# Starting a hand-written engine order three units earlier, and a vote in two steps

## The chip, the cores and the metric

One core of a Trainium2 chip. The metric is the device time of one execution in microseconds, the median of several runs.

## What is computed

```python
state = np.zeros((B, H, D, D))                      # (4, 8, 48, 48)
for t in range(S):                                  # 768
    kt, vt, rt, wt = (k[:, :, t], v[:, :, t], r[:, :, t], w[:, :, t])
    cur = np.einsum('bhd,bhe->bhde', u[None] * kt, vt)
    y[:, :, t] = np.einsum('bhd,bhde->bhe', rt, state + cur)
    state = wt[:, :, :, None] * state + np.einsum('bhd,bhe->bhde', kt, vt)
x = y.transpose(0, 2, 1, 3).reshape(B * S, H * D)   # (3072, 384)
h = x @ w_in                                        # w_in (384, 2048)
out = (h * np.cos(h)) @ w_out                       # w_out (2048, 384)
```

A linear attention with a decaying state, and behind it a two-layer network whose gate is h cos h. All of it is in float32.

## The kernel before

**Chunks.** The sequence is cut into 24 chunks of 128 steps (4 batches of 6). For each chunk the tile tt holds r, k and w; v and rk (r and k once more, with time on the partitions) are loaded apart. `att_decay` turns the decays into products: e, a backward scan on VectorE (L225); f, a reciprocal and a forward scan (L230, L232); then r and k are multiplied by the scans' results (steps r, L237, and k, L238). `att_diag` makes the diagonal of the scores: m and u multiply rk by k and by u (L250, L251), c sums over each head (L255), and GpSimd spreads the sums out (L265). TensorE computes scores (pa, L288), transposes of k (pt, L301; step K copies them to kn), the new state (pst, L323; step n adds the old one) and the outputs (py, L355 to L374); P puts the scores into their triangle (L292), X splits the outputs in a high and a low part, xT (L148). The step d multiplies the state of the chunk before (L278), and four small copies on ScalarE place it in past.

**Units.** Two chunks make a block of 256 columns of the network, and a block has 8 units of 256 columns of w_in. For a unit t, mm1 makes ph with 18 matmuls in three passes of split precision (L443); the gate follows: I rounds (ScalarE, L405), S reduces (VectorE, L408), N is the sine (ScalarE, L421), M multiplies with ph (VectorE, L422), H takes the high part (ScalarE, L145) and L the low part (GpSimd, L148, two instructions). mm2 then adds 12 matmuls to acc (L462), two units later (`LAG`). Only two PSUM banks hold ph in this part, so mm1 of unit t waits for M of unit t-2.

**Weights.** Each pair of weight blocks is loaded raw and split by ScalarE and VectorE (lines 155 to 176) once, in the first 106 us, between units 0 and 15, which belong to blocks 0 and 1 in the order `PAIR`.

**Order.** In the rows `START` the events of the first units are written out, by hand for TensorE alone; the other engines' order there comes from the scheduler, by priorities. After `START` the order of TensorE, VectorE, ScalarE and GpSimd is the order of the code, and SyncE's is the scheduler's. There `events` reads one row of `PLAN` for each unit t; "k+5" is step k of chunk 2i + 5, where i is t // 8; e, m and the like put a part of a step at that place, and t+2 has TensorE transpose a chunk. Before, `START` has five rows that end with unit 15, and the rows by hand begin with unit 16; only its third (n = 2) differs from `PLAN`. The dictionaries `EARLY` and `LATER` say which engine does what in the two phases: in `EARLY` rk is multiplied on GpSimd and kn copied on ScalarE, in `LATER` both on VectorE.

**Vote.** At the end the largest |w| and the smallest product of decays decide whether the result stands or a slow loop runs. `take_vote` is called behind unit slots-4: VectorE makes vote, least and low (L568 to L572), TensorE sums them over the partitions (L574, L575), VectorE makes a number of it.

Of the kernel before, what the change touches and what calls it, by code (L numbers as in the profile page):

```python
# [9 lines left out]
F32 = mybir.dt.float32  # L10
# [7 lines left out]
ALU = mybir.AluOpType  # L18
ET = mybir.EngineType

C = 128
# [4 lines left out]
R = ROW + HD  # L26
# [26 lines left out]
PLAN = ["t+2 t+3 load+6 mm1 K+2 K+3 e+4 I S k+4 N M mm2 H L f+4",  # L53
# [7 lines left out]
START = ["load0 load1 f lv0 decay0 f diag0 a0 lv1 decay1 diag1 a1 w load2 f w o0 x0 decay2 diag2 m0 m1",  # L61
# [4 lines left out]
FIRST = {2: "mm1 a+2 a+3 I S m+4 N M P+2 P+3 mm2 H L"}  # L66
LAST = "mm1 I S N M", "mm1 I S N M mm2 h l", "mm2 h l"
CHECK = 14
PAIR = "0001110101010101"
# [1 line left out]
             o="a lv", s="t d lv", p="o d")  # L71
# [3 lines left out]
def rwkv_cos_ffn(ctx: ExitStack, tc: tile.TileContext, tr, tn, tv, u, ut, wts, w, rkw, vst, us, xs, out):  # L75
    nc = tc.nc
# [8 lines left out]
    cst = ctx.enter_context(tc.tile_pool(name="cst", bufs=1))  # L85
# [6 lines left out]
    def bank(kind, shape, name):  # L92

        tags = BANKS[stage[0]]
        turn[kind] += 1
        return ps.tile(shape, F32, tag=tags[kind][turn[kind] % len(tags[kind])], name=name)
# [3 lines left out]
    def buf(tag, shape, dtype, name=None, pool=sb):  # L100
# [16 lines left out]
                            axis=mybir.AxisListType.X, op=ALU.add)  # L117
# [5 lines left out]
    ones = cst.tile([128, 1], F32, name="ones")  # L123
# [7 lines left out]
    raw, wgt, last = {}, {}, {}  # L131

    E = {}
# [256 lines left out]
    def check_decays(n):  # L390

        ww = buf("tt", [128, w.shape[1] // WCH], F32, "ww")
        nc.sync.dma_start(out=ww, in_=w[:, n * w.shape[1] // WCH:(n + 1) * w.shape[1] // WCH])
        top = buf("top", [128, 1], F32)
        nc.vector.tensor_reduce(out=top, in_=ww, axis=mybir.AxisListType.X, op=ALU.max, apply_absolute_value=True)
        nc.vector.tensor_tensor(out=wmax, in0=wmax, in1=top, op=ALU.max)
# [86 lines left out]
    NU = NF // FU  # L483
# [3 lines left out]
    for i in PAIR:  # L487
# [3 lines left out]
    slots = len(seq)  # L491
# [4 lines left out]
                 a=att_scores, t=att_transpose, s=att_state, o=att_own, p=att_past, x=att_x)  # L496
# [37 lines left out]
    def up(n):  # L534

        if n == 0 and up1[0] < slots:
            if up1[0] - up1[1] > LAG + 1:
                up(1)
            mm1(up1[0])
            up1[0] += 1  # L540
        elif n == 1 and up1[1] < up1[0]:
            mm2(up1[1])
            up1[1] += 1

    def events(i, row, t):
        for e in row.split():
            n, _, d = e.partition("+")
            if e == "mm1":
                up(0)
            elif e == "mm2":  # L550
                if up1[1] <= t - LAG:
                    up(1)
            elif e in "ISNMHLhl":
                at = (e.upper(), t - e.islower())
                if at in parts:
                    parts.pop(at)()
            elif n in "efrkmucPKXn":
                at = i * (1 if n in "Xn" else BLK) + int(d)
                for m in dict(e=("decay",), m=("diag",)).get(n, ()):
                    att(at, m)  # L560
                if (n, at) in parts:
                    parts.pop((n, at))()
            else:
                att(i * (1 if n in "osp" else BLK) + int(d), n)

    def take_vote():
        vote = cst.tile([128, 1], F32, name="vote")
        nc.vector.tensor_single_scalar(out=vote, in_=wmax, scalar=1.0, op=ALU.is_gt)  # L568
        least = cst.tile([R, 1], F32, name="least")
        nc.vector.tensor_reduce(out=least, in_=wholes.rearrange("p g a -> p (g a)"), axis=mybir.AxisListType.X, op=ALU.min)  # L570
        low = cst.tile([R, 1], F32, name="low")
        nc.vector.tensor_single_scalar(out=low, in_=least, scalar=LEAST, op=ALU.is_le)  # L572
        pv = bank("a", [C, 512], "pv")
        nc.tensor.matmul(out=pv[:1, 0:1], lhsT=vote, rhs=ones[:, 0:1], start=True, stop=True)  # L574
        nc.tensor.matmul(out=pv[:1, 1:2], lhsT=ones[:R, 0:1], rhs=low, start=True, stop=True)  # L575
        votes = cst.tile([1, 1], F32, name="votes")
        nc.vector.tensor_reduce(out=votes, in_=pv[:1, 0:2], axis=mybir.AxisListType.X, op=ALU.add)
        nc.vector.tensor_copy(out=bad, in_=votes)

    bad = cst.tile([1, 1], I32, name="bad")  # L580

    up1 = [0, 0]
# [15 lines left out]
    with tc.manual_schedule(engines={ET.PE, ET.DVE, ET.Activation, ET.Pool}):  # L598
        up2 = up1[0]
        for t in range(up2, slots + LAG):  # L600
            n = t % NU
            if t == slots - 2:
                E["g0"] = nc.vector
            row = FIRST[n] if t < up2 + NU and n in FIRST else PLAN[n]
            events(t // NU, row if t < slots - 2 else LAST[t - slots + 2] if t <= slots else "mm2", t)
            if t >= slots - CHECK and n_checked[0] < WCH:
                check_decays(n_checked[0])
                n_checked[0] += 1
            if t == slots - 4:
                take_vote()  # L610
        while up1[1] < slots:
            up(1)
    assert not parts, list(parts)
# [159 lines left out]
```

## Time and profile before

| what | value |
|---|---|
| median of 3 runs | 538.82 us (538.73 to 540.53) |
| the profiled execution, its own time | 538.93 us |
| its span in the profile | 537.2 us |
| TensorE busy | 503.7 us, 94% |
| VectorE busy | 378.9 us, 71% |
| ScalarE busy | 274.2 us, 51% |
| GpSimd busy | 212.9 us, 40% |

The span reaches from the first to the last instruction; the 1.7 us between it and the execution's own time lie around it. Busy is the time in which the engine executes something, as a share of the span. An engine that is not busy may wait for another one, and a busy engine may be busy with nothing that the end waits for, so the shares alone don't say which engine sets the time.

### The profile page before, as it was taken

The page shows a single profiled execution, that of the slowest core. Times are in us where ns is not written, and L with a number is a line of the kernel's source. Part 1 is how long each engine was busy: PE and PEld are TensorE (multiplying, and loading weights), DVE is VectorE, ACT ScalarE, POOL GpSimd, SP SyncE. Part 2 cuts the span into 40 slices and gives each one's busy share as a digit, 9 for nine tenths or more (in the row PEclk, how much of TensorE's full clock was granted, in tenths as well). Part 3 has the DMA queues.
Part 4 walks back from the last instruction along what each step waited for, and adds up shares of the span by engine and source line. Part 5 has one row for each costly group of instructions (what it writes and reads, how often), then busy time and mean ns, then how long its engine had stood idle before and what let it go on. Part 6 is the DMA issues. An engine that isn't in the chain of part 4 may idle for free.

```text
span 537.2 us, 11909 instructions
## 1 busy us (share of the span) xinstructions
PE 503.7 (94%) x4964; PEld 485.7 (90%) x4964; DVE 378.9 (71%) x570; ACT 274.2 (51%) x454; POOL 212.9 (40%) x274
## 2 busy tenths in 40 slices
PE   3657999969999999999999999999999999999997
PEld 3656898958999999999999999999999999999987
DVE  7998999864746946946946946946946946678433
ACT  1788999635535435444434435435434444444543
POOL 4161346744323524524524524524524524423320
PEclk9878999999999999999999999999999999999999
DMA  8994851214142132133132123123123120050000
GB/s 272 315 322 133 270 188 57 63 60 136 64 116 54 60 109 59 60 96 74 60 95 74 60 79 91 60 70 100 59 63 115 60 97 23 31 177 1 31 2 32
DMA packets 16728, 52.17 MB, mean 97 GB/s; under 512 B 2016, under 2 KB 8416, under 8 KB 16672
## 3 DMA queue, kind: packets, MB, share of 16 engines
q1 hardware_dynamic: 16528, 51.28, 31.1%
q8 instruction: 40, 0.66, 0.5%
q14 instruction: 16, 0.13, 0.1%
q10 hardware_dynamic: 144, 0.10, 0.1%
HBM read 46.65 MB, written 4.72 MB: 96 GB/s over the span
## 4 chain that ended last, share of the span: by engine, by line
PE 77%; DVE 13%; ACT 4%; issue 2%; POOL 2%; DMA 1%; DVEq 0%; ACTq 0%; POOLq 0%
PE ph L443 33%; PE acc L462 32%; PE pa L288 4%; DVE h L173 2%; PE py L355 2%; DVE w L148 2%; PE py L360 2%; PE pst L323 2%; DVE rr L422 1%; DVE ee L225 1%; DVE tt L232 1%; PE py L374 1%; DVE rr L408 1%; PE pt L301 1%; DVE tt L237 1%
## 5 line engine op out<-in xcount | busy, mean ns | idle before, releaser
L148 POOL TENSOR_TENSOR gs<-rr,gs 128x256 fp32r<-128x256 f32 x188 | 155.1, 846 | 245.4 <-ACT gs L145 245.4
L443 PE MATMUL ph<-xT,w 128*128 128x256 f32 x1728 | 224.4, 284 | 11.5 <-ACT w L145 5.2
L443 PEld LDWEIGHTS ph<-xT,w 128*128 128x128 f32 x1728 | 215.2, 190 | 15.6 <-ACT w L145 5.6
L462 PE MATMUL acc<-w,gs 128*128 128x384 f32 x1152 | 217.3, 338 | 1.1 <-DVE rr L422 1.0
L462 PEld LDWEIGHTS acc<-w,gs 128*128 128x128 f32 x1152 | 195.9, 188 | 2.5 <-issue 1.2
L408 DVE SCALAR_TENSOR_TENSOR rr<-rr,ph 128x512 f32<-128x512 int32 x96 | 65.6, 683 | 85.3 <-ACT rr L405 84.8
L421 ACT ACTIVATE rr<-rr,quarter 128x512 f32<-128x512 f32 x96 | 69.4, 723 | 89.8 <-DVE rr L408 89.6
L145 ACT CAST gs<-rr 128x512 fp32r<-128x512 f32 x96 | 59.6, 621 | 66.3 <-DVE rr L422 39.1
L422 DVE TENSOR_TENSOR rr<-rr,ph 128x512 f32<-128x512 f32 x96 | 65.7, 684 | 29.1 <-ACT rr L421 29.0
L405 ACT ACTIVATE rr<-ph 128x512 int32<-128x512 f32 x96 | 57.3, 597 | 54.3 <-PE ph L443 53.7
L265 POOL TENSOR_SCALAR_AFFINE_SELECT asb<-cd 128x512 f32<-128x512 f32 x48 | 42.8, 915 | 60.4 <-DVE cd L255 40.9
L225 DVE TENSOR_TENSOR_SCAN ee<-tt,one_e 112x516 f32<-112x516 f32 x24 | 33.1, 1381 | 1.6 <-DMA tt<-tr 1.6
L292 DVE COPY_PREDICATED asb<-mask,pa 128x512 f32<-128x512 uint8 x48 | 31.7, 727 | 1.3 <-PE pa L288 1.3
L148 DVE TENSOR_TENSOR xT<-py,xT 128x384 fp32r<-128x384 f32 x24 | 12.2, 551 | 26.1 <-ACT xT L145 26.1
L232 DVE TENSOR_TENSOR_SCAN tt<-tt,inj 112x516 f32<-112x516 f32 x24 | 30.1, 1254 | 0.6
L288 PE MATMUL pa<-tt 48*128 48x128 f32 x384 | 28.2, 299 | 0.0
L288 PEld LDWEIGHTS pa<-tt 48*128 48x128 f32 x384 | 25.0, 205 | 2.8 <-issue 2.2
L244 PEld LDWEIGHTS pc<-u_by_head,rkt 112*128 112x128 f32 x48 | 8.3, 262 | 14.7 <-DVE rkt L219 8.4
L244 PE MATMUL pc<-u_by_head,rkt 112*128 112x2 f32 x48 | 8.7, 303 | 13.5 <-DVE rkt L219 12.9
L237 DVE TENSOR_TENSOR tt<-tt 112x512 f32<-112x512 f32 x24 | 21.0, 875 | 0.1
L145 ACT COPY past<-dd 48x192 f32<-48x192 f32 x40 | 14.0, 350 | 13.7 <-DVE dd L278 11.3
L238 DVE TENSOR_TENSOR tt<-tt,ee 112x512 f32<-112x512 f32 x24 | 20.0, 835 | 0.0
(68 smaller groups left out, 345.6 us busy)
## 6 DMA issues: line engine op xcount, KB each, us to landing
tt<-tr SPq DMA_DIRECT2D x22, 674.2 KB, 7.0
raw<-wts SPq DMA_DIRECT2D x16, 768.0 KB, 6.0
rk<-tn SPq DMA_DIRECT2D x18, 384.0 KB, 3.3
v<-tv SPq DMA_DIRECT2D x24, 224.0 KB, 5.9
ww<-w SPq DMA_DIRECT2D x6, 768.0 KB, 5.1
out<-ob SPq DMA_DIRECT2D x23, 192.0 KB, 2.0
tt<-tr SPq DMA_DIRECT2D x4, 224.0 KB, 4.7
tt<-tr SPq DMA_DIRECT2D x2, 226.2 KB, 3.8
```

The costliest lines, as they stand in the source:

```text
L145: (nc.scalar.copy if E[name] is nc.scalar else E[name].tensor_copy)(out=out, in_=in_)
L148: E[name].tensor_tensor(out=out, in0=full, in1=high.bitcast(F32), op=ALU.subtract)
L225: nc.vector.tensor_tensor_scan(out=ee.rearrange("p a t -> p (a t)")[:, ::-1], data0=wp[:, 1:W129 + 1][:, ::-1], data1=one_e.rearrange("p a ...
L232: nc.vector.tensor_tensor_scan(out=wp[:, 0:W129], data0=wp[:, 0:W129], data1=inj.rearrange("p a t -> p (a t)"), initial=0.0, op0=ALU.mult, ...
L265: nc.gpsimd.affine_select(out=asb, in_=col.unsqueeze(2).to_broadcast([C, NP, C]), pattern=[[0, 4], [1, C]], compare_op=ALU.is_equal, fill= ...
L288: nc.tensor.matmul(out=pa[h][:, p], lhsT=a["k3"][rows(h), p], rhs=a["r3"][rows(h), p], start=True, stop=True)
L405: nc.scalar.activation(made["rr"].bitcast(I32), ph, AF.Copy, scale=INV2PI / W_SCALE, bias=0.25)
L408: nc.vector.scalar_tensor_tensor(out=made["rr"], in0=made["rr"].bitcast(I32), scalar=-2.0 * math.pi * W_SCALE, in1=ph, op0=ALU.mult, op1=A ...
L421: N=lambda: nc.scalar.activation(made["rr"], made["rr"], AF.Sin, scale=1.0 / W_SCALE, bias=quarter),
L422: M=lambda: nc.vector.tensor_tensor(out=made["rr"], in0=made["rr"], in1=ph, op=ALU.mult), H=high, L=low)
L443: nc.tensor.matmul(out=ph[:, fi], lhsT=wgt[u * FU + fi][:, 0, a, kt * 128:(kt + 1) * 128], rhs=xT[:, b, kt], start=n == 0, stop=n == 3 * K ...
L462: nc.tensor.matmul(out=accs[i][j][:, :DM], lhsT=gs[:, a, fi, j * C:(j + 1) * C], rhs=wgt[u * FU + fi][:, 1, b], start=u == 0 and fi == 0 a ...
```

## The change

The fifth row of `START` is taken away, so that the order by hand begins with unit 13. `FIRST` becomes a list of seven rows for units 13 to 19, and from unit 20 on `PLAN` is used. The copies kn are made on ScalarE in units 13 to 15. `take_vote` is split: the operations of VectorE come behind unit slots-5, the matmuls and what follows behind unit slots-4, as before.

```diff
-         "mm2 m0 m1 lr6 lr7 diag6 decay6 mm2 t4 t5 m0 m1 lv6 lv7 diag7 decay7 s2 mm2 o2 p2 load8 lr8 lr9 m0 m1 x4 mm2 load9 d6 d7 lv8 lv9"]
-FIRST = {2: "mm1 a+2 a+3 I S m+4 N M P+2 P+3 mm2 H L"}
+FIRST = ["mm2 lr+4 lr+5 mm1 load+6 I S e+4 N M mm2 H L k+4",
+         "t+2 t+3 mm1 K+2 K+3 f+4 I S s+1 n+1 N M mm2 H L r+4 m+4 u+4",
+         "o+1 p+1 mm1 load+7 c+4 lr+6 X+1 I S e+5 N M mm2 H L k+5 f+5 m+5 lv+6 lv+7 d+4 d+5",
+         "t+2 t+3 mm1 K+2 K+3 r+3 I S u+3 N M mm2 H L c+3 lr+5 load+6 e+4",
...
-    def take_vote():
+    def take_vote(last):
+        if last:
+            pv = bank("a", [C, 512], "pv")
+            nc.tensor.matmul(out=pv[:1, 0:1], lhsT=told["vote"], rhs=ones[:, 0:1], start=True, stop=True)
+            nc.tensor.matmul(out=pv[:1, 1:2], lhsT=ones[:R, 0:1], rhs=told["low"], start=True, stop=True)
...
+            return
...
-            n = t % NU
+            n = t - up2
+            E["kn"] = nc.scalar if n < 3 else nc.vector
...
-            row = FIRST[n] if t < up2 + NU and n in FIRST else PLAN[n]
+            row = FIRST[n] if n < len(FIRST) else PLAN[t % NU]
...
-            if t == slots - 4:
-                take_vote()
+            if t in (slots - 5, slots - 4):
+                take_vote(t == slots - 4)
```

TensorE's order is the same instruction for instruction. In the changed kernel all lines behind the table stand 5 lines lower (L408 is L413, L422 is L427, L225 is L230, L238 is L243), those behind `take_vote` 9.

First place: VectorE between the gates of units 11 and 13, before. rr_1068 is unit 11, rr_1133 unit 12 and rr_1195 unit 13; tt_1162 is chunk 7, rk_1206 its rk.

```order
L422 TENSOR_TENSOR rr_1068<-rr_1068,ph_1049 128x512
L225 SCALAR_TENSOR_TENSOR ee_1289<-tt_1162,one_e_77 112x516
L255 TENSOR_REDUCE cd_1283<-rk_1206 128x8
L230 RECIPROCAL inj_80<-ee_1289 112x4
L238 TENSOR_TENSOR tt_1162<-tt_1162,ee_1289 112x512
L232 SCALAR_TENSOR_TENSOR tt_1162<-tt_1162,inj_80 112x516
L237 TENSOR_TENSOR tt_1162<-tt_1162 112x512
L408 SCALAR_TENSOR_TENSOR rr_1133<-rr_1133,ph_1114 128x512
L422 TENSOR_TENSOR rr_1133<-rr_1133,ph_1114 128x512
L408 SCALAR_TENSOR_TENSOR rr_1195<-rr_1195,ph_1176 128x512
```

The same place in the changed kernel (rr_1204 is unit 13, tt_1099 chunk 6):

```order
L427 TENSOR_TENSOR rr_1068<-rr_1068,ph_1049 128x512
L297 COPY_PREDICATED asb_1035<-mask_75,pa_1088 128x512
L413 SCALAR_TENSOR_TENSOR rr_1133<-rr_1133,ph_1114 128x512
L427 TENSOR_TENSOR rr_1133<-rr_1133,ph_1114 128x512
L413 SCALAR_TENSOR_TENSOR rr_1204<-rr_1204,ph_1183 128x512
L230 SCALAR_TENSOR_TENSOR ee_1207<-tt_1099,one_e_77 112x516
L427 TENSOR_TENSOR rr_1204<-rr_1204,ph_1183 128x512
```

Six instructions of chunk 7 between M of unit 11 and S of unit 12 are gone, the sum over rk among them, whose products GpSimd made; chunk 6's backward scan, which stood ahead of unit 8's M, comes in unit 13.

Second place: VectorE from the gate of unit 15 on, before (rr_1419 is unit 15, kn_1486 and kn_1488 the transposed k of chunks 6 and 7) and then in the changed kernel (rr_1401 is unit 15).

```order
L408 SCALAR_TENSOR_TENSOR rr_1419<-rr_1419,ph_1400 128x512
L422 TENSOR_TENSOR rr_1419<-rr_1419,ph_1400 128x512
L145 COPY kn_1486<-pt_1455 128x384
L145 COPY kn_1488<-pt_1460 128x384
L225 SCALAR_TENSOR_TENSOR ee_1490<-tt_1392,one_e_77 112x516
```

```order
L413 SCALAR_TENSOR_TENSOR rr_1401<-rr_1401,ph_1367 128x512
L230 SCALAR_TENSOR_TENSOR ee_1404<-tt_1162,one_e_77 112x516
L427 TENSOR_TENSOR rr_1401<-rr_1401,ph_1367 128x512
L243 TENSOR_TENSOR tt_1162<-tt_1162,ee_1404 112x512
L235 RECIPROCAL inj_80<-ee_1404 112x4
L237 SCALAR_TENSOR_TENSOR tt_1162<-tt_1162,inj_80 112x516
L255 TENSOR_TENSOR rk_1181<-rk_1181 128x384
L283 TENSOR_TENSOR dd_1433<-sn_773,ee_1207 112x192
L283 TENSOR_TENSOR dd_1437<-sn_775,ee_1404 112x192
L150 COPY kn_1470<-pt_1441 128x384
L150 COPY kn_1472<-pt_1446 128x384
```

Chunk 7's scan, its multiplication of k, which TensorE transposes at the start of unit 16, and seven more instructions now stand around M of unit 15.

Third place: VectorE around the vote, before (rr_6046 is unit slots-4) and in the changed kernel (rr_6052).

```order
L422 TENSOR_TENSOR rr_6006<-rr_6006,ph_5987 128x512
L408 SCALAR_TENSOR_TENSOR rr_6046<-rr_6046,ph_6027 128x512
L422 TENSOR_TENSOR rr_6046<-rr_6046,ph_6027 128x512
L568 TENSOR_SCALAR vote_6067<-wmax_87 128x1
L570 TENSOR_REDUCE least_6069<-wholes_86 112x1
L572 TENSOR_SCALAR low_6071<-least_6069 112x1
L577 TENSOR_REDUCE votes_6076<-pv_6073 1x1
```

```order
L427 TENSOR_TENSOR rr_6006<-rr_6006,ph_5987 128x512
L581 TENSOR_SCALAR vote_6027<-wmax_87 128x1
L583 TENSOR_REDUCE least_6029<-wholes_86 112x1
L585 TENSOR_SCALAR low_6031<-least_6029 112x1
L413 SCALAR_TENSOR_TENSOR rr_6052<-rr_6052,ph_6033 128x512
L427 TENSOR_TENSOR rr_6052<-rr_6052,ph_6033 128x512
L577 TENSOR_REDUCE votes_6076<-pv_6073 1x1
```

Three operations moved from behind unit slots-4's gate to ahead of it.

## Rows read from the trace of the kernel before

**Rows 1.** Windows: busy us and instructions per engine, TensorE's clock, DMA share, GB/s.

```profile
88.00:124.00 36.00, 29.32 (x238) 26.90 (x237) 27.55 (x40) 19.90 (x34) 22.50 (x22) 1.00 0.22 67
151.00:172.00 21.00, 21.00 (x267) 20.30 (x266) 12.37 (x21) 9.04 (x17) 7.40 (x10) 1.00 0.40 108
```

**Rows 2.** TensorE's timeline, 88 to 122 us: start, duration, instruction, [idle before, releaser].

```profile
88.83 2.35 PE L462 MATMUL acc<-w,gs 128*128 128x384 f32 x12
91.36 2.37 PE L443 MATMUL ph<-xT,w 128*128 128x256 f32 x18 [0.18 <-DVE rr L422]
94.34 1.05 PE L244 MATMUL pc<-u_by_head,rkt 112*128 112x2 f32 x8 [0.62 <-DVE asb L292]
...
105.00 2.25 PE L462 MATMUL acc<-w,gs 128*128 128x384 f32 x12
108.42 2.34 PE L443 MATMUL ph<-xT,w 128*128 128x256 f32 x18 [1.17 <-DVE rr L422]
110.59 2.92 PE L462 MATMUL acc<-w,gs 128*128 128x384 f32 x12
113.36 0.93 PE L301 MATMUL pt<-ident,tt 112*128 112x112 f32 x8
117.48 2.36 PE L443 MATMUL ph<-xT,w 128*128 128x256 f32 x18 [3.19 <-DVE rr L422]
120.46 0.67 PE L323 MATMUL pst<-v,kn 128*64 128x48 f32 x16 [0.62 <-ACT kn L145]
121.90 0.67 PE L323 MATMUL pst<-v,kn 128*64 128x48 f32 x16 [0.78 <-ACT kn L145]
```

**Rows 3.** TensorE's timeline in an undisturbed stretch, 170 to 174 us.

```profile
170.56 2.25 PE L462 MATMUL acc<-w,gs 128*128 128x384 f32 x12
172.65 0.93 PE L301 MATMUL pt<-ident,tt 112*128 112x112 f32 x8
173.35 2.35 PE L443 MATMUL ph<-xT,w 128*128 128x256 f32 x18
```

**Rows 4.** VectorE's timeline, four rows between 96 and 117 us.

```profile
96.89 1.78 DVE L232 TENSOR_TENSOR_SCAN tt<-tt,inj 112x516 f32<-112x516 f32 x1
...
108.20 1.22 DVE L225 TENSOR_TENSOR_SCAN ee<-tt,one_e 112x516 f32<-112x516 f32 x1
111.35 0.55 DVE L255 TENSOR_REDUCE cd<-rk 128x8 f32<-128x384 f32 x1 [1.93 <-POOL rk L251]
...
116.65 0.69 DVE L422 TENSOR_TENSOR rr<-rr,ph 128x512 f32<-128x512 f32 x1 [0.79 <-ACT rr L421]
```

**Rows 5.** GpSimd's timeline at 96.8 us, the two subtractions of a gate.

```profile
96.76 2.45 POOL L148 TENSOR_TENSOR gs<-rr,gs 128x256 fp32r<-128x256 f32 x2 [2.42 <-ACT gs L145]
```

**Rows 6.** The timeline of all engines near the end, around the vote.

```profile
510.95 2.26 PE L443 MATMUL ph<-xT,w 128*128 128x256 f32 x18
...
512.74 1.43 POOL L148 TENSOR_TENSOR gs<-rr,gs 128x256 fp32r<-128x256 f32 x2 [2.76 <-ACT gs L145]
...
513.05 2.25 PE L462 MATMUL acc<-w,gs 128*128 128x384 f32 x12
...
513.95 0.69 DVE L408 SCALAR_TENSOR_TENSOR rr<-rr,ph 128x512 f32<-128x512 int32 x1 [2.02 <-ACT rr L405]
...
516.24 0.19 PE L574 MATMUL pv<-ones,vote 128*1 128x1 f32 x2 [0.94 <-DVE vote L568]
...
516.59 0.19 PE L575 MATMUL pv<-low,ones 112*1 112x1 f32 x2 [0.16 <-DVE low L572]
...
516.70 2.37 PE L443 MATMUL ph<-xT,w 128*128 128x256 f32 x18
```

**Rows 7.** VectorE's groups by line and shape, 125 to 500 us: busy, mean ns | idle before.

```profile
L225 DVE TENSOR_TENSOR_SCAN ee<-tt,one_e 112x516 f32<-112x516 f32 x16 | 21.9, 1367 | 0.0
...
L238 DVE TENSOR_TENSOR tt<-tt,ee 112x512 f32<-112x512 f32 x16 | 13.2, 825 | 0.0
```

**Rows 8.** DMA issues of the page: KB each, median us to landing.

```profile
tt<-tr SPq DMA_DIRECT2D x22, 674.2 KB, 7.0
```

More of the change, by code (lines that the diff above doesn't have):

```diff
@@ L564, in events @@
                 att(i * (1 if n in "osp" else BLK) + int(d), n)
-    def take_vote():
-        vote = cst.tile([128, 1], F32, name="vote")
+    def take_vote(last):
[3 more added lines that the diff above has]
+            nc.tensor.matmul(out=pv[:1, 1:2], lhsT=ones[:R, 0:1], rhs=told["low"], start=True, stop=True)
+            votes = cst.tile([1, 1], F32, name="votes")
+            nc.vector.tensor_reduce(out=votes, in_=pv[:1, 0:2], axis=mybir.AxisListType.X, op=ALU.add)
+            nc.vector.tensor_copy(out=bad, in_=votes)
+            return
+        told["vote"] = vote = cst.tile([128, 1], F32, name="vote")
         nc.vector.tensor_single_scalar(out=vote, in_=wmax, scalar=1.0, op=ALU.is_gt)
@@ L570, in take_vote @@
         nc.vector.tensor_reduce(out=least, in_=wholes.rearrange("p g a -> p (g a)"), axis=mybir.AxisListType.X, op=ALU.min)
-        low = cst.tile([R, 1], F32, name="low")
+        told["low"] = low = cst.tile([R, 1], F32, name="low")
         nc.vector.tensor_single_scalar(out=low, in_=least, scalar=LEAST, op=ALU.is_le)
[L573 to L578, printed above, removed]
+    told = {}
     bad = cst.tile([1, 1], I32, name="bad")
```

5 rows, old and new, of tables (FIRST, START) are left out of this document.

## The prediction

> **What bounds the kernel now.** First the windows: over most of the run TensorE has no idle time, and the stretch from 88 to 124 us is the exception. From 151 to 172 us TensorE is busy for all 21 us; from 88 to 124 us only for 29.32 of 36 us, at a granted clock of 1.00 in both [rows 1]. So the clock is not the reason; something makes TensorE wait, and it is only worth while to work where it waits.
>
> Second, TensorE's timeline in that stretch, read as steps from the start of one row to the start of the next, against the same steps in the undisturbed stretch. There a unit's twelve L462 matmuls take 2.09 us until the next row starts (170.56 to 172.65), eight transposes 0.70 (172.65 to 173.35) [rows 3], and eighteen L443 matmuls 2.10 (510.95 to 513.05) [rows 6]. In the bad stretch [rows 2]:
> - L462 at 88.83 to L443 at 91.36: 2.53, so 0.44 lost
> - L443 at 91.36 to L244 at 94.34: 2.98, 0.88 lost
> - L462 at 105.00 to L443 at 108.42: 3.42, 1.33 lost
> - L462 at 110.59 to the transposes at 113.36: 2.77, 0.68 lost
> - the transposes at 113.36 to L443 at 117.48: 4.12 against 0.70, 3.42 lost
> - L443 at 117.48 to L323 at 120.46: 2.98, 0.88 lost
> - inside L323, before 121.90: 0.78 lost
>
> Together **8.41 us**, which agrees with the 6.68 us not busy in the window [rows 1]: a stalled row is also drawn longer, so the steps show a little more. Three of the waits before L443 carry "DVE rr L422": L443 of unit t needs the PSUM bank that the gate of unit t-2 reads last, in M (L422).
>
> Third, VectorE's timeline, to see why M is late. Before M at 116.65 it ran the backward scan of chunk 7 (108.20), then waited 1.93 us at 111.35 for GpSimd's multiplication of rk, and only then came to the rest of chunk 7's attention work [rows 4]. VectorE executes in the order of its queue, so the two gate steps of unit 12 stood behind work that TensorE needed only for the transposes of unit 16, four units later. That is the 3.42.
>
> **The change part by part.**
>
> *Units 13 to 15, and the rows to unit 19.* TensorE's own order does not move by a single row; what moves is VectorE, ScalarE, GpSimd and four loads. The first piece of order shows that the scans and multiplications of chunks 6 and 7, both sums over rk and their GpSimd products are gone from between the gate steps S and M of units 11 to 13. With them gone, M of unit 12 waits only for its own sine, and the wait on GpSimd at 111.35 disappears because rk is multiplied on VectorE, later. The 3.42, the 0.88 and the 0.78 (copies kn on ScalarE stood behind the late gate of unit 12) have no cause left. The 0.44, 0.88, 1.33 and 0.68 came while VectorE still prepares the last weights; there the changed order takes out two scans and two multiplications of 512 columns (chunk 6), one of the scans drawn out to 1.78 us [rows 4]. I take it that 0.4 of these 3.33 us stays, since the weight work stays; the bounds are 0 and 3.33. Term: **-8.41 + 0.4**.
>
> *A new wait at unit 16.* The work has to be done somewhere. The second piece of order shows chunk 7's: backward scan e after S of unit 15, then M, then the multiplication k; and TensorE's row of unit 16 begins with the transposes of exactly that k. From rows of the steady state: L443 starts at 510.95 and ends 2.26 later, at 513.21; S of its gate ends at 513.95 + 0.69 = 514.64, so 1.43 after it [rows 6]. Then the scan, 1.37 on average, and k, 0.83 [rows 7], with M, 0.69 [rows 4], between: 1.43 + 1.37 + 0.69 + 0.83 = 4.32 us after the end of L443. TensorE meanwhile has one unit of L462 and chunk 6's half of the transposes: it arrives 2.10 + 2.09 + 0.35 = 4.54 after the start of L443, 2.28 after its end. So it waits 4.32 - 2.28 = **+2.04 us**. Bounds: 1.75 with a scan of 1.22 as at 108.20 [rows 4] and a k as short as M; 3.2 with a scan of 1.78 and a k that first waits 0.72 for one GpSimd subtraction (half of the 1.43 that two take [rows 6]).
>
> *The vote.* Now vote, least and low stand on VectorE behind M of unit n-4 and two matmuls on TensorE wait for them: L462 at 513.05 to L443 at 516.70 is 3.65 us instead of 2.09. The two small matmuls stay; they took 0.46 from 516.24 to the next L443 at 516.70, of which 0.16 is the second one's wait for low, so 0.30 is left [rows 6]. In the third piece of order the three operations stand a unit earlier, ahead of S; VectorE is idle for 2.02 us there [rows 6], which hides their half microsecond; without that cover they would cost that much. Term: **-(3.65 - 2.09 - 0.30) = -1.26**, between -1.10 and -1.56.
>
> *At nothing:* rk's four products on VectorE go into its idle time in units 14 to 16, as they do in every later block; GpSimd only loses work. The copies kn of chunks 4 and 5 stay on ScalarE, which is busy for 19.90 of 36 us even in the bad window, and those of chunks 6 and 7 go to VectorE, as before [rows 1]. If that cover fails, the price is in the rivals.
>
> Sum: 538.93 (the profiled execution's own time; span 537.2) - 8.41 + 0.4 + 2.04 - 1.26 = 531.7. The median of the runs is 0.11 below the profiled execution, so **531.6 us**. No later stretch can take the gain back, since TensorE is not kept waiting there [rows 1], and it does the same work in the same order.
>
> *A rule weighed.* The profile shows a scan that started 0.13 us after a GpSimd subtraction and took 1.78 [rows 4], against 1.22 for another; the pair of subtractions took 2.45 [rows 5] against 1.43 [rows 6]. The Trainium skill ("SBUF — State Buffer", section "SBUF: two separate sides") says that VectorE instructions with two SBUF inputs and GpSimd exclude each other from a port pair, the one that comes second being blocked for the whole of the other instruction. These rows agree with it: 1.22 and the rest of one subtraction (half of 1.43, less the 0.13) make 1.81. By the rule the new wait could be longer than the sum has it; this is the second rival.
>
> **The rivals.**
>
> *The weight work was the cause up to 113 us.* VectorE is busy for 27.55 of the 36 us [rows 1], and the preparation of the last weight blocks stays on it. If all of 0.44 + 0.88 + 1.33 + 0.68 stays, only 5.08 goes: 538.93 - 5.08 + 2.04 - 1.26 = 534.6. Against it: what is taken out is of the size of the waits, and M stands nearer to S.
>
> *GpSimd blocks the chain of chunk 7.* If both the scan and k of unit 15 begin behind a GpSimd subtraction, each grows by up to 0.72: the new wait is 3.5 and the time 533.1. Against it: in the changed order the subtraction of unit 15 becomes ready only after M and ScalarE's high part, when k has already begun.
>
> *Slower.* In SyncE's queue the load of rk of chunk 8 stands ahead of the big loads tt of chunks 8 and 9, and it takes the buffer that the sum over rk of chunk 6 reads, which now comes in unit 15. The scan of chunk 8 at the end of unit 16 waits for that tt, and S of unit 17 stands behind it. From the sum to the scan lie two units of TensorE and the new wait, 2 x 4.19 + 2.04 = 10.4 us; a tt lands 7.0 us after its issue [rows 8]. So 3.4 us are left. For a time above 538.93 the load would have to take 3.4 + 7.2 = 10.6 us longer than 7.0; from there each microsecond is one of time. The DMA engines move little in this stretch (share 0.22 [rows 1]), which speaks against it.
>
> *It does not do what it says:* the new waits of unit 16 and later eat all that is freed, and the time stays within 0.5%. It would take 7 us of waits where the rows account for 2.
>
> **How the numbers follow.** Forecast 0.63 (own range 530.9 to 532.5); weight work 0.13; GpSimd 0.12; no change 0.03; slower 0.02; better than forecast, with the new wait hidden by something I do not see (529.7), 0.07. The range of 530.0 to 534.8 takes in the forecast and the first two rivals. 0.5% of 538.8 is 2.7 us, about what a measurement of this kernel can tell from no change; under 536.1 lie the forecast, two rivals and the better case, 0.95; no change 0.03; slower 0.02.
>
> **What would show it right or wrong.** Right: L443 follows L462 without "DVE rr L422" from 88 to 124 us, and TensorE's transposes near 125 us show a wait of about 2 us for VectorE's multiplication by the backward scan; the steps around the vote matmuls shrink to about 2.4 us. Wrong, if waits before L443 or L462 remain before 113 us (first rival), if the wait at the transposes is over 3 us with a scan or multiplication of over 1.4 us in front (second), or if VectorE's scan of chunk 8 waits for its load (slower).

## The result and the profile after

| | before | changed |
|---|---|---|
| median | 539.38 us (4 runs, 538.73 to 540.53) | 531.22 us (4 runs, 530.97 to 531.41) |
| span of the profiled execution | 537.2 us | 529.5 us |
| GpSimd busy | 212.9 us | 206.8 us |

The ratio is 0.9846, with a 95% interval of 0.9826 to 0.9866. Faster was forecast, 531.6 us in a range of 530.0 to 534.8. The forecast stood on three runs of the kernel before; the fourth, 539.94 us, moves that median from 538.82 to 539.38.

The window of the bad stretch, to be read against [rows 1]:

```profile
88.00:124.00 36.00, 36.00 (x387) 34.63 (x387) 26.59 (x40) 22.95 (x39) 17.27 (x22) 1.00 0.27 85
```

TensorE is busy for all 36 us, where it was for 29.32. Its timeline in the changed kernel, from the place of [rows 2] to unit 16 (start, duration, instruction, idle before):

```profile
89.36 2.35 PE L467 MATMUL acc<-w,gs 128*128 128x384 f32 x12
91.56 2.26 PE L448 MATMUL ph<-xT,w 128*128 128x256 f32 x18
93.66 0.95 PE L249 MATMUL pc<-u_by_head,rkt 112*128 112x2 f32 x8
...
104.23 2.25 PE L467 MATMUL acc<-w,gs 128*128 128x384 f32 x12
106.32 2.26 PE L448 MATMUL ph<-xT,w 128*128 128x256 f32 x18
108.41 2.25 PE L467 MATMUL acc<-w,gs 128*128 128x384 f32 x12
110.50 0.93 PE L306 MATMUL pt<-ident,tt 112*128 112x112 f32 x8
111.20 2.35 PE L448 MATMUL ph<-xT,w 128*128 128x256 f32 x18
113.48 1.13 PE L328 MATMUL pst<-v,kn 128*64 128x48 f32 x32
...
119.77 2.37 PE L448 MATMUL ph<-xT,w 128*128 128x256 f32 x18
121.98 2.25 PE L467 MATMUL acc<-w,gs 128*128 128x384 f32 x12
124.06 0.55 PE L306 MATMUL pt<-ident,tt 112*128 112x112 f32 x4
125.92 0.58 PE L306 MATMUL pt<-ident,tt 112*128 112x112 f32 x4 [1.31 <-issue]
```

No step up to 113.48 has a wait in it: L467 to L448 2.09 us (104.23 to 106.32), L467 to the transposes 2.09, the transposes to L448 0.70, L448 to L328 2.28. What is left of the 8.41 us is 0.11 at 89.36 and 0.18 before L328, and the profile marks neither as a wait: 119.77 to 121.98, also behind smaller matmuls, is 2.21 us, and the 2.28 before L328 comes back where the copies kn are on another engine (last experiment). One wait is new: the second four transposes start 1.86 us after the first four, 0.35 of which is their own work, so 1.51 us.

VectorE's timeline ahead of that wait:

```profile
122.81 0.69 DVE L413 SCALAR_TENSOR_TENSOR rr<-rr,ph 128x512 f32<-128x512 int32 x1 [1.40 <-ACT rr L410]
123.42 1.22 DVE L230 TENSOR_TENSOR_SCAN ee<-tt,one_e 112x516 f32<-112x516 f32 x1
124.56 0.66 DVE L427 TENSOR_TENSOR rr<-rr,ph 128x512 f32<-128x512 f32 x1
125.14 0.68 DVE L243 TENSOR_TENSOR tt<-tt,ee 112x512 f32<-112x512 f32 x1
```

S, chunk 7's scan, M and k follow each other without a gap; k ends at 125.82, and TensorE goes on at 125.92.

Around the vote (the places of [rows 6], TensorE's rows):

```profile
506.61 2.25 PE L467 MATMUL acc<-w,gs 128*128 128x384 f32 x12
...
508.79 0.19 PE L574 MATMUL pv<-ones,vote 128*1 128x1 f32 x2
...
508.96 2.37 PE L448 MATMUL ph<-xT,w 128*128 128x256 f32 x18
```

The step is 2.35 us and was 3.65: 1.30 less.

The steps add up to -8.41 + 0.29 + 1.51 - 1.30 = -7.9 us; the medians differ by 8.16, the spans by 7.7. Taken as one stretch up to unit 15's first matmuls, the account closes. In the kernel before these are at

```profile
127.72 2.37 PE L443 MATMUL ph<-xT,w 128*128 128x256 f32 x18
```

so 38.89 us after the L462 at 88.83 [rows 2]; in the changed kernel it is 119.77 - 89.36 = 30.41 us, 8.48 less. The changed kernel's profiled execution comes to this stretch 0.53 us later (89.36 for 88.83), and -8.48 + 1.51 - 1.30 + 0.53 = -7.74 us is the difference of the spans.

### The profile page after: what moved, and what is told of

Its sections match the earlier page's. It is cut to its first block, busy times and chain, and to the rows that moved or that the text cites. A ratio compares the mean times of both kernels' runs of the same rounds, so it can differ in the third digit from the quotient of the medians.

```text
span 529.5 us, 11906 instructions
## 1 busy us (share of the span) xinstructions
PE 505.6 (95%) x4964; PEld 488.9 (92%) x4964; DVE 380.1 (72%) x574; ACT 273.8 (52%) x454; POOL 206.8 (39%) x270
## 4 chain that ended last, share of the span: by engine, by line
PE 84%; DVE 11%; ACT 2%; issue 1%; DMA 1%; DVEq 0%
PE ph L448 36%; PE acc L467 35%; PE pa L293 4%; PE py L360 2%; DVE w L153 2%; PE py L365 2%; DVE h L178 2%; PE pst L328 2%; DVE ee L230 1%; PE pt L306 1%; PE py L379 1%; DVE tt L237 1%; DVE rr L427 1%; DVE h L177 1%; PE py L375 1%
## 5 line engine op out<-in xcount | busy, mean ns | idle before, releaser
L153 POOL TENSOR_TENSOR gs<-rr,gs 128x256 fp32r<-128x256 f32 x188 | 156.8, 854 | 244.8 <-ACT gs L150 244.8
L448 PE MATMUL ph<-xT,w 128*128 128x256 f32 x1728 | 225.1, 284 | 4.4 <-ACT w L150 3.0
L448 PEld LDWEIGHTS ph<-xT,w 128*128 128x128 f32 x1728 | 216.2, 191 | 7.9 <-ACT w L150 3.5
L467 PE MATMUL acc<-w,gs 128*128 128x384 f32 x1152 | 216.8, 337 | 1.0 <-DVE rr L427 1.0
L467 PEld LDWEIGHTS acc<-w,gs 128*128 128x128 f32 x1152 | 196.1, 188 | 1.7 <-issue 1.2
L413 DVE SCALAR_TENSOR_TENSOR rr<-rr,ph 128x512 f32<-128x512 int32 x96 | 65.5, 683 | 81.5 <-ACT rr L410 80.9
L427 DVE TENSOR_TENSOR rr<-rr,ph 128x512 f32<-128x512 f32 x96 | 65.6, 684 | 28.5 <-ACT rr L426 28.3
L270 POOL TENSOR_SCALAR_AFFINE_SELECT asb<-cd 128x512 f32<-128x512 f32 x48 | 40.1, 858 | 61.2 <-DVE cd L260 41.0
L230 DVE TENSOR_TENSOR_SCAN ee<-tt,one_e 112x516 f32<-112x516 f32 x24 | 32.4, 1350 | 1.7 <-DMA tt<-tr 1.7
L249 PEld LDWEIGHTS pc<-u_by_head,rkt 112*128 112x128 f32 x48 | 9.1, 282 | 14.0 <-DVE rkt L224 8.5
L249 PE MATMUL pc<-u_by_head,rkt 112*128 112x2 f32 x48 | 9.3, 316 | 13.0 <-DVE rkt L224 13.0
L150 ACT CAST xT<-py 128x384 fp32r<-128x384 f32 x24 | 10.4, 482 | 16.2 <-PE py L379 15.5
```

The source lines that it names most:

```text
L150: (nc.scalar.copy if E[name] is nc.scalar else E[name].tensor_copy)(out=out, in_=in_)
L153: E[name].tensor_tensor(out=out, in0=full, in1=high.bitcast(F32), op=ALU.subtract)
L230: nc.vector.tensor_tensor_scan(out=ee.rearrange("p a t -> p (a t)")[:, ::-1], data0=wp[:, 1:W129 + 1][:, ::-1], data1=one_e.rearrange("p a ...
L270: nc.gpsimd.affine_select(out=asb, in_=col.unsqueeze(2).to_broadcast([C, NP, C]), pattern=[[0, 4], [1, C]], compare_op=ALU.is_equal, fill= ...
L413: nc.vector.scalar_tensor_tensor(out=made["rr"], in0=made["rr"].bitcast(I32), scalar=-2.0 * math.pi * W_SCALE, in1=ph, op0=ALU.mult, op1=A ...
L427: M=lambda: nc.vector.tensor_tensor(out=made["rr"], in0=made["rr"], in1=ph, op=ALU.mult), H=high, L=low)
```

## The experiments

Each was timed against the kernel before on the same chip; medians and ratios to it are given. The kernel before took 538.96 us beside the first four and 539.22 us beside the last three.

### The vote alone

The kernel before, with `take_vote(last)` and its two calls from the diff above, and nothing else of it.

> The kernel before with the vote alone in two steps; rows and engines as before. Theory: the two vote matmuls wait for VectorE's vote, least and low behind M, and nothing else is slow there, so the step from L462 to the next L443 around them falls from 3.65 to about 2.35 us, the steps from 88 to 124 us keep their 8.4 us of waits, and the time is 1.3 us under the kernel before (ratio 0.9976). Rival: the matmuls themselves, their weights of one column and the change of PSUM bank, make up most of the 3.65; then the step stays over 3 us and the gain is under 0.5.

Measured: 537.70 against 538.96 us, ratio 0.9976 (0.9966 to 0.9985). TensorE's timeline:

```profile
108.90 2.34 PE L443 MATMUL ph<-xT,w 128*128 128x256 f32 x18 [1.15 <-DVE rr L422]
...
117.56 2.34 PE L443 MATMUL ph<-xT,w 128*128 128x256 f32 x18 [3.20 <-DVE rr L422]
```

```profile
513.12 2.25 PE L462 MATMUL acc<-w,gs 128*128 128x384 f32 x12
...
515.47 2.37 PE L443 MATMUL ph<-xT,w 128*128 128x256 f32 x18
```

The step around the vote is 2.35 us, as forecast, and the waits in the middle stay. The small matmuls themselves cost 2.35 - 2.09 = 0.26 us; what cost 1.3 us was that their operands were made behind M.

### The rows alone

```diff
-            if t in (slots - 5, slots - 4):
-                take_vote(t == slots - 4)
+            if t == slots - 4:
+                take_vote()
```

`take_vote` itself is that of the kernel before again.

> The changed kernel with the vote in one step again. Theory: 1.3 us slower than the changed kernel, so about 6.9 us under the kernel before (ratio 0.987); no wait of TensorE from 88 to 124 us, 1.5 us at the transposes of unit 16, and 3.65 us around the vote matmuls. Rival: the two parts are not additive because TensorE's gain in the middle moves the end's work against SyncE's loads and the vote; then the step around the vote differs from 3.65 by over 0.5.

Measured: 532.21 us, ratio 0.9875 (0.9861 to 0.9890).

```profile
506.24 2.25 PE L467 MATMUL acc<-w,gs 128*128 128x384 f32 x12
509.43 0.19 PE L579 MATMUL pv<-ones,vote 128*1 128x1 f32 x2 [0.94 <-DVE vote L573]
...
509.90 2.37 PE L448 MATMUL ph<-xT,w 128*128 128x256 f32 x18
```

3.66 us around the vote again: the two parts add up. Some 6.7 us are the rows', 1.3 the vote's.

### Chunk 7's scan and multiplication ahead

```diff
-         "o+1 p+1 mm1 load+7 c+4 lr+6 X+1 I S e+5 N M mm2 H L k+5 f+5 m+5 lv+6 lv+7 d+4 d+5",
+         "o+1 p+1 mm1 load+7 c+4 lr+6 e+5 X+1 I S k+5 N M mm2 H L f+5 m+5 lv+6 lv+7 d+4 d+5",
```

> The changed kernel with chunk 7's backward scan ahead of the split of the outputs in unit 15's row and its multiplication k right after S; nothing else moves. Theory (the wait at the transposes is VectorE's queue: S, scan, M, k in a row): the scan falls into the 1.75 us in which VectorE waits for ScalarE, k is done some 0.7 us after S, the wait of 1.5 us at the transposes goes and the time falls by 1.3 to 1.5 us below the changed kernel (about 0.982 of the kernel before). Rival: the load of chunk 7, or the multiplication beside GpSimd, holds k back; then over 1 us of the wait stays. Another rival: M of unit 15, now behind k, is late and TensorE's L443 of unit 17 waits for it; then a wait of like size appears there.

Measured: 529.49 us, ratio 0.9821 (0.9808 to 0.9833), the fastest of all. The interval touches that of the changed kernel, which was timed at another time; beside the run without the vote, timed with it, it is 532.21 - 529.49 = 2.72 us, of which the vote is 1.3 and 1.4 is left. VectorE's and then TensorE's timeline:

```profile
118.44 1.22 DVE L230 TENSOR_TENSOR_SCAN ee<-tt,one_e 112x516 f32<-112x516 f32 x1
120.28 1.02 DVE L153 TENSOR_TENSOR xT<-py,xT 128x384 fp32r<-128x384 f32 x2 [0.61 <-ACT xT L150]
122.70 0.69 DVE L413 SCALAR_TENSOR_TENSOR rr<-rr,ph 128x512 f32<-128x512 int32 x1 [1.40 <-ACT rr L410]
123.30 0.69 DVE L243 TENSOR_TENSOR tt<-tt,ee 112x512 f32<-112x512 f32 x1
```

```profile
123.95 0.93 PE L306 MATMUL pt<-ident,tt 112*128 112x112 f32 x8
124.65 2.35 PE L448 MATMUL ph<-xT,w 128*128 128x256 f32 x18
```

The scan lies in VectorE's wait for ScalarE, which shrinks from 1.75 to 0.61 us; k is done at 123.99, and the eight transposes take their plain 0.70 us. M of unit 15 is not late: no wait appears behind it. The profile of the changed kernel names no releaser for the 1.31 ("issue"); with k done at 123.99 and not at 125.82 the wait is gone, so it was k.

### rk on VectorE, in the scheduler's order

The kernel before, with one line in `att_diag`:

```diff
             rk = a["rk"][:, 0]
+            E["rk"] = E["ru"] = nc.vector
```

> The kernel before with one difference: the products over rk of chunks 6 and 7 are made on VectorE and not on GpSimd; the order is still the scheduler's. It takes away the wait of VectorE for GpSimd (1.93 us at 111.35, 2.03 at 104.38) and the two products between GpSimd's subtractions, and puts four of 0.55 us into VectorE's queue. Theory one (the queue's order is the cause, GpSimd only adds to it): the wait of 3.42 us at L443 of unit 14 shrinks to about 2.7, the 1.33 and 0.68 shrink, and the gain is about 3 us (ratio 0.994), less than half of the change's. Theory two (GpSimd's products were the cause, the order hardly matters): the waits at 105 to 117 us go wholly, and the gain is 5 us or more. Theory three (VectorE is simply full there): four more products make it slower.

Measured: 535.75 us, ratio 0.9941 (0.9927 to 0.9956). TensorE's timeline:

```profile
91.82 2.37 PE L444 MATMUL ph<-xT,w 128*128 128x256 f32 x18 [0.17 <-DVE rr L423]
94.80 1.05 PE L244 MATMUL pc<-u_by_head,rkt 112*128 112x2 f32 x8 [0.61 <-DVE asb L293]
...
105.47 2.25 PE L463 MATMUL acc<-w,gs 128*128 128x384 f32 x12
107.56 2.26 PE L444 MATMUL ph<-xT,w 128*128 128x256 f32 x18
109.66 2.25 PE L463 MATMUL acc<-w,gs 128*128 128x384 f32 x12
111.75 0.93 PE L302 MATMUL pt<-ident,tt 112*128 112x112 f32 x8
114.12 2.34 PE L444 MATMUL ph<-xT,w 128*128 128x256 f32 x18 [1.44 <-DVE rr L423]
117.10 0.67 PE L324 MATMUL pst<-v,kn 128*64 128x48 f32 x16 [0.64 <-ACT kn L145]
```

Theory one holds, with its size off. The 1.33 and the 0.68 are gone (two steps of 2.09), so they were GpSimd's products; the 3.42 has become 2.37 - 0.70 = 1.67, not 2.7; the 0.44, the two of 0.88 and the 0.78 stay. About half of the 3.42 was the wait for GpSimd, the other half chunk 7's decays in the queue. VectorE was not full: four more products made the kernel 3.2 us faster.

GpSimd's part includes a wait for a load. In the kernel before, its first product of chunk 7 waits for the load of rk before it starts, and the gate's two subtractions stand behind the products:

```profile
108.25 1.98 POOL L250 TENSOR_TENSOR rk<-rk 128x384 f32<-128x384 f32 x1 [1.79 <-DMA rk<-tn]
```

In this run VectorE waits 0.15 us for the same load. How much of GpSimd's part is the load's and how much the engine's, no run separates.

### Chunk 6's decays in the first phase again

```diff
-... m0 m1 w a5 load6 mm2 m0 m1 w d4 d5 load7"]
+... m0 m1 w a5 load6 decay6 mm2 m0 m1 w d4 d5 load7"]
```

> The changed kernel with chunk 6's decays (two scans, two multiplications, reciprocal) given back to the first phase, where the scheduler places them among the weight work; chunk 7's stay in unit 15, rk stays on VectorE. Theory: the 0.44, 0.88, 1.33 and 0.68 us up to 113 us came from chunk 6's decays and from GpSimd's products together; with the decays back, a wait of 0.6 to 1 us before L249 (near 94 us) returns and little else, and the time is 0.5 to 1 us above the changed kernel. Rival: the scans alone made all 3.3 us; then 2.5 us or more return. Second rival: the weight work made them; that is excluded already if they are gone in the changed kernel.

Measured: 532.34 us, ratio 0.9869 (0.9847 to 0.9890), 1.1 us above the changed kernel. TensorE's timeline:

```profile
91.40 2.26 PE L448 MATMUL ph<-xT,w 128*128 128x256 f32 x18
94.42 1.05 PE L249 MATMUL pc<-u_by_head,rkt 112*128 112x2 f32 x8 [0.76 <-DVE asb L297]
...
114.75 1.13 PE L328 MATMUL pst<-v,kn 128*64 128x48 f32 x32 [0.23 <-ACT kn L150]
```

0.92 us before L249 came back (3.02 against 2.10) and 0.3 before L328, nothing of the 1.33 and the 0.68. So the 0.88 before L249 comes with chunk 6's decays, of which only the backward scan stands ahead of P there (the forward scan starts at 97.57). The 0.44 did not come back, and VectorE's timelines show why, of the kernel before and then of this run:

```profile
86.32 0.89 DVE L278 TENSOR_TENSOR dd<-sn,ee 112x192 f32<-112x192 f32 x1
...
89.07 1.66 DVE L225 TENSOR_TENSOR_SCAN ee<-tt,one_e 112x516 f32<-112x516 f32 x1
```

```profile
86.67 1.77 DVE L230 TENSOR_TENSOR_SCAN ee<-tt,one_e 112x516 f32<-112x516 f32 x1
...
102.82 0.35 DVE L283 TENSOR_TENSOR dd<-sn,ee 112x192 f32<-112x192 f32 x1
```

Before, both the multiplication dd of chunk 5 and the scan stood ahead of the M (90.65) that the L443 at 91.36 waits for. Here the scheduler put dd behind it, and VectorE, which has no gap there, comes to M at 90.28, early enough for the L448 at 91.40; in the changed kernel it is the scan that is gone and dd that stays. So the 0.44 needed both, and the run doesn't give chunk 6's decays back at quite their old places.

### rk on GpSimd, at the new places

```diff
             E["kn"] = nc.scalar if n < 3 else nc.vector
+            E["rk"] = E["ru"] = nc.gpsimd if n < 4 else nc.vector
```

> The changed kernel with the products over rk of chunks 6 and 7 on GpSimd again, at their new places behind the gates. Theory (place, not engine): they stand where nothing waits for them soon, and the time is the changed kernel's within 0.5 us. Rival (engine): VectorE waits for GpSimd at the sums c again, the gate steps behind are late, and the time rises by 1 us or more, with a wait before L448 of units 16 to 18.

Measured: 531.22 us, ratio 0.9846 (0.9825 to 0.9867), the changed kernel's time. VectorE's timeline:

```profile
121.53 0.56 DVE L260 TENSOR_REDUCE cd<-rk 128x8 f32<-128x384 f32 x1 [4.22 <-POOL rk L256]
122.00 1.01 DVE L153 TENSOR_TENSOR xT<-py,xT 128x384 fp32r<-128x384 f32 x2
```

VectorE waits 4.22 us for GpSimd, over twice as long as the 1.93 of [rows 4], and TensorE loses nothing: the split of the outputs comes later, but only unit 16 needs it. At this place the engine makes no difference; at the old one it made 3.2 us. What cost those 3.2 us was GpSimd's products at a place without slack.

### The copies kn on VectorE

```diff
-            E["kn"] = nc.scalar if n < 3 else nc.vector
```

> The changed kernel with the copies kn of units 13 to 15 on VectorE, as in all later units. Theory: VectorE's queue in unit 14 has room, the state matmuls of block 1 wait 0.3 us at most, and the time is the changed kernel's within 0.5 us. Rival: the copies stand behind the forward scan of chunk 6 and the state matmuls wait for over 1 us.

Measured: 531.01 us, ratio 0.9843 (0.9823 to 0.9864). No wait before the state matmuls: L448 to L328 is 2.28 us (111.16 to 113.44), as in the changed kernel. This line of the change is worth nothing that can be measured.

## Why the prediction was right

**The waits from 88 to 124 us.** Right: they are gone, and without VectorE's work of chunks 6 and 7 ahead of the gates. That the sum left 0.4 us of the 8.41 and the runs 0.29 is luck: the 0.4 was for waits behind the weight work, of which none stayed, and the 0.29 is not marked as a wait: steps of 2.20 and 2.28 us, behind smaller matmuls, stand where the sum took 2.09 and 2.10. The prediction laid the first four waits on chunk 6 and the weight work together; the runs divide them otherwise. The 0.88 before L249 was chunk 6's backward scan (it returns with the decays), the 0.44 that scan and a dd together, the 1.33 and the 0.68 were GpSimd's products over rk (they go when only those move), and of the 3.42 about half was GpSimd, half chunk 7's decays. The 0.88 and the 0.78 at L323 are not divided: in the changed kernel the gate of unit 12 is early and the copies kn stand ahead of ScalarE's rounding of unit 14, where before they stood behind its sine and its high part of unit 13, and no run moves one without the other. The first rival, the weight work, is excluded: it is still there, and the waits are not.

**The new wait at unit 16.** Right in place and cause, shown by the run that moves k; its size was off, 1.51 us against 2.04, and under the lower bound of 1.75. The step that failed is "1.43 + 1.37 + 0.69 + 0.83 = 4.32 us after the end of L443". That end is 119.77 + 2.37 = 122.14, and k ended at 125.82, 3.68 us later. The scan took 1.22 instead of the mean 1.37 and k 0.68 instead of 0.83, and each VectorE instruction started about 0.08 us before the end of the one ahead (123.42 after 122.81 + 0.69 = 123.50), which a sum of durations leaves out three times; S ended 1.36 us after L443 and not 1.43, and M took 0.66 and not 0.69. Together that is 0.64 us; 0.10 us the other way, from the end of k to the transposes, stood in no term. The means of [rows 7] contain instructions that were drawn out beside GpSimd; here none was running.

**The second rival**, GpSimd blocking that chain, did not come: the subtraction of unit 15 began at 126.03, after k, as was argued against it.

**The vote.** Right: 1.30 us against 1.26, and alone it takes 0.24% off the time.

**At nothing.** The copies kn and the engine of rk's products are worth nothing, as two runs show. The prediction put rk's move to VectorE among the things that cost nothing; that is so at the new place, but at the old one the same move gains 3.2 us.

**Slower** and **no change** did not come; no wait of VectorE for a load shows in its rows from 86 to 140 us. The scan of chunk 8 began at 133.23, 14.6 us after the sum over rk of chunk 6 ended (118.63), where the prediction counted 10.4.

**The sum.** With the measured terms it would have been 538.93 - 8.41 + 0.29 + 1.51 - 1.30 = 531.0, and by the median 530.9. That 531.6 came within 0.4 us of 531.22 is in part luck: the new wait was forecast 0.53 us too long, and the profiled execution of the changed kernel comes half a microsecond later to the bad stretch. The L448 ahead of it starts at 86.01, and in the vote's run, which has the old order there, at 85.95; in the execution shown of before it was 85.47. That is ahead of the first moved instruction.

## What to carry to other kernels

Measure a stalled stretch as steps from row to row against the same steps where nothing waits, and then ask of the engine that comes late what stands ahead in its queue and when that is needed: here instructions of 0.2 to 1.8 us, right in themselves, cost 8 us because they stood ahead of a gate, though the results of most were needed only units later. The same waiting moved to a place with slack cost nothing (4.22 us of it), so an engine's idle time and an engine's choice say little without the place. When work is moved, follow the chain to its first reader; here it ended 1.5 us late, and a scan put into an idle gap ahead gave that back: 529.49 us.

## What the runs showed of the hardware

GpSimd's pair of subtractions, 1.43 us alone, took 3.00 us in the changed kernel beside VectorE's forward scan and products, while the scan took its 1.23; then the two multiplications dd, 0.35 us each where GpSimd was quiet, took 1.70 together. The first row is of the kernel before, the others of the changed one:

```profile
123.52 0.35 DVE L278 TENSOR_TENSOR dd<-sn,ee 112x192 f32<-112x192 f32 x1
```

```profile
126.03 3.00 POOL L153 TENSOR_TENSOR gs<-rr,gs 128x256 fp32r<-128x256 f32 x2 [5.52 <-ACT gs L150]
```

```profile
125.94 1.23 DVE L237 TENSOR_TENSOR_SCAN tt<-tt,inj 112x516 f32<-112x516 f32 x1
127.09 0.53 DVE L255 TENSOR_TENSOR rk<-rk 128x384 f32<-128x384 f32 x1
127.55 1.70 DVE L283 TENSOR_TENSOR dd<-sn,ee 112x192 f32<-112x192 f32 x2
```

The one that began first was not slowed and the other was, which agrees with the rule weighed in the prediction (the Trainium skill, "SBUF — State Buffer", section "SBUF: two separate sides"). From the pair's start at 126.03 to the end of VectorE's product at 127.62 are 1.59 us, and with the pair's own 1.43 that makes 3.02, close to the 3.00 measured. Here it cost nothing: TensorE shows no wait behind them up to 140 us.

TensorE's granted clock in the first 60 us differs between the two profiled executions, though the order up to 60 us is the same in all nine profiles: from 20 to 40 and from 40 to 60 us it is 0.76 and 0.90 in the execution shown of before, 0.59 and 0.81 in that of the changed kernel. The half microsecond by which the latter is later at 86 us goes with it over these profiles: where the clock from 20 to 60 us is 0.83, this row of TensorE starts at 85.47; where it is 0.79 (four profiles), at 85.63 to 85.93; where it is 0.70 (four), at 85.95 to 86.31. With one profile of each kernel that is no proof of a cause.
